# Loading the layer-normed x of a block with its rows repeated by the DMA, in place of copies by ScalarE and GpSimd

## The chip, the cores and the metric

The kernel runs on one core of one Trainium2 chip. The metric is the device time of one execution in microseconds (us), so lower is better. Before the change it is 2559.25 us, the median of 3 runs (2558.43 to 2561.18).

## The reference

One layer norm feeds two branches, multi-head attention and a GEGLU feed-forward network; their product gates the output. All arrays are float32: x is 2048 tokens by D = 576, there are 32 heads of 18 elements, and the feed-forward width is F = 4608.

```python
xn = layernorm(x)
q, k, v = split(xn @ wqkv)                     # 32 heads of 18
s = (softmax(q k^T / sqrt(18)) v) @ wo         # branch A
g = silu((gelu(xn @ w_gate) * (xn @ w_up)) @ w_down)   # branch B
return x + s * g
```

## The kernel before

Float32 products are made of reduced-precision pieces: a tile is split into a high part and a low part (x = hi + lo), and a product takes hi*hi, lo*hi and hi*lo.

The 2048 tokens are cut into NB = 4 blocks of TB = 512. A **prologue** (to about 198 us) norms and transposes each block's x, splits it (hi, lo), projects q, k and v, and stores q, k, v and also the transposed x itself: `store_xt` (L273) writes block b to a DRAM array `xhs[b]`, shaped [2 (hi, lo), 576 features, 512 tokens], so a feature's 512 tokens are one run of 2 KB.

The **main part** consists of sections (`section`, L578). A section makes one tile of 128 gate columns and 128 up columns for one token block: 27 pairs of matmuls (9 chunks of 64 features, 3 products each). A pair uses the upper and the lower half of TensorE's rows at once: gate weights stand in partitions 0 to 63, up weights in 64 to 127, and since both halves multiply the same x, the x chunk must stand in both halves of the partitions (L431, `rr = slice(HR * a, HR * a + HR)`). Between the pairs stand the score matmuls of the attention (L814 and L861), behind them the sums over values (L878) and, after every second section, the down projection (L542). TensorE's order is written out by hand, and so is the order of SP's DMA queue in the main part; in the prologue a scheduler places everything except TensorE's work.

A token block lasts 36 sections. Its x stands in SBUF as six tiles `xd0_k` (hi) and `xd1_k` (lo), k = 0, 1, 2, each [128 partitions, 3 chunks, 512 tokens], 768 KB, with a single buffer. So at a block's end, in its last section, the next block's tiles are loaded as the old ones fall free: k = 0 behind pair 9, k = 1 behind pair 18, k = 2 behind pair 27 (hooks at L606 to L608, and L620). Pairs 0 to 8 of the next section need k = 0, pairs 9 to 17 need k = 1, pairs 18 to 26 need k = 2. There are three such block ends, at about 727, 1327 and 1928 us.

Before the change `load_xd` (L146) loads k = 0 and k = 1 into the lower 64 partitions only, and engines copy them to the upper 64: ScalarE the hi tiles, GpSimd the lo tiles (`copy_xd`, L157). For k = 2 the load is issued twice, once for each half. Block 0 is loaded in the prologue, lower halves only, and GpSimd copies all six tiles (L388 to L391).

All DMAs are issued by SP, in order, on one queue. Each carries one of eight completion counters in turn, so SP can issue a request only when the request eight places ahead of it has landed.

Two other places matter below. In the prologue `project` (L314) writes its result to tiles t1 and t2 with three buffers, which SP stores to DRAM (`qk<-t`, L321), from a PSUM tile `po` with three buffers. And `load_scale` (L702) loads sums of the softmax with four rows of DRAM, each repeated for 32 partitions:

```python
o, d = spare()
nc.sync.dma_start(o[:, i, 0:TB], oT[g, :, cols])
nc.sync.dma_start(d[:, i, 0:TB], rT[QD * g:QD * g + QD, cols].rearrange("h (o s) -> h o s", o=1).to_broadcast([QD, 32, TB]))
```

The first fills 128 partitions from 128 rows, the second fills 128 partitions from 4 rows; each lands 256 KB.

Of the kernel before, what the change touches and what calls it, by code (L numbers as in the profile page):

```python
# [8 lines left out]
F32 = mybir.dt.float32  # L9
F32R = mybir.dt.float32r  # L10
AF = mybir.ActivationFunctionType
# [5 lines left out]
S, D, H, DH, F = 2048, 576, 32, 18, 4608  # L17
P = 128
NT = S // P
TB = 512  # L20
NB = S // TB
KT = 4
R0 = KT * P
HR = 64
NC = D // HR
XG = 3
NG = NC // XG
# [41 lines left out]
def gu_part(n):  # L69
    return G * part(*divmod(n // G, NR)) + n % G  # L70


def f(ap):
    return ap.bitcast(F32)
# [14 lines left out]
def kernel(ctx: ExitStack, tc: tile.TileContext, x, wqkv, wo, w_gate, w_up, w_down, out):  # L89
    nc = tc.nc  # L90
    x = x.rearrange("b s d -> (b s) d")
# [3 lines left out]
    dram = ctx.enter_context(tc.tile_pool(name="dram", bufs=1, space=DRAM))  # L95
# [9 lines left out]
    ys = dram.tile([S - TB, D], F32, name="ys")  # L105
    zeros = dram.tile([2, 2 * TB], F32, name="zeros")
    ts = dram.tile([NR, P, 2 * 7 * DC], F32, name="ts")
    xhs = [dram.tile([2, D, TB], F32, name=f"xhs{b}") for b in range(NB)]

    ident = const.tile([P, P], F32, name="ident")  # L110
    make_identity(nc, ident)
# [31 lines left out]
        w[1].append(hi)  # L143
        w[2].append(lo)

    def load_xd(b, k, halves=1):  # L146

        out = []
        for i in range(2):
            t = wts.tile([P, XG, TB], F32R, name=f"xd{i}_{k}")  # L150
            for a in range(halves):
                nc.sync.dma_start(f(t)[HR * a:HR * a + HR],
                                  xhs[b][i, k * XG * HR:(k + 1) * XG * HR, :].rearrange("(k p) t -> p k t", p=HR))
            out.append(t)
        return out

    def copy_xd(x, part, keep=lambda i: i, i=slice(None)):  # L157

        if part == 0:
            keep(nc.scalar.activation(x[0][HR:P, i], f(x[0])[0:HR, i], AF.Copy))  # L160
        else:
            keep(nc.gpsimd.tensor_copy(x[1][HR:P, i], x[1][0:HR, i]))


    def after(what, before, reason):
        tc.add_manual_dep(what.ins, before.ins.name, mybir.DependencyInfo(
            mybir.DependencyClass.Sync, mybir.DependencyReason.DATA), reason=reason)
# [7 lines left out]
    with tc.tile_pool(name="pro", bufs=1) as pro, tc.tile_pool(name="pps", bufs=1, space=PSUM) as pps:  # L175
# [34 lines left out]
        def load_x(b):  # L210
            keep = tc.keep_in_program_order if b == 1 else lambda i: i
            xr = []
            for j in range(4):
                xx = pro.tile([P, D + HR], F32, name="xx", bufs=4)
                keep(nc.sync.dma_start(xx[:, 0:D], x[b * TB + j * P:b * TB + (j + 1) * P, :]))
                xr.append(xx)
            return xr
# [43 lines left out]
        def transposes(b, xr):  # L261
            xt = XT[b % 2]
            pts = [pps.tile([P, TB], F32, name="pt", bufs=KT + 1) for k in range(KT + 1)]
            for j in range(4):
                if b == 0 and j == 0:
                    warm(46)
                for k in range(KT + 1):
                    nc.tensor.transpose(pts[k][:, j * P:(j + 1) * P], xr[j][:, k * P:(k + 1) * P], ident)  # L268
            for k in range(KT + 1):
                split_t(pts[k], k, xt)  # L270
            return xt

        def store_xt(b, xt):  # L273
            keep = tc.keep_in_program_order if b == 0 else lambda i: i
            for i in range(2):
                keep(nc.sync.dma_start(xhs[b][i, 0:R0, :].rearrange("(k p) t -> p k t", p=P), f(xt[i])))
                keep(nc.sync.dma_start(xhs[b][i, R0:D, :], f(xt[2])[HR * i:HR * i + HR, :]))

        XT = [(pro.tile([P, KT, TB], F32R, name=f"xth{i}"), pro.tile([P, KT, TB], F32R, name=f"xtl{i}"),
               pro.tile([P, TB], F32R, name=f"xtr{i}")) for i in range(2)]  # L280
# [10 lines left out]
        def load_qk(t, keep=lambda i: i):  # L291
            return t, load_rows(t * P, P, keep)
# [4 lines left out]
        def split_qk(t, raw):  # L297
            hi, lo = (pro.tile([P, KT, P], F32R, name=f"q{m}{t}") for m in "hl")
            first = split(hi, lo, raw)
            put_qk(t, hi, lo)  # L300
            return first
# [31 lines left out]
        t = ORDER[0]  # L333
# [26 lines left out]
        xt = transposes(0, xr)  # L360
        for c0 in (slice((t + 1) * P, 2 * D), slice(0, t * P)):
            split_av(QR[0][:, c0], QR[1][:, c0], raw_r[:, c0], tc.keep_in_program_order)
        for b in range(NB):
            for n, t in enumerate(ORDER):
                if b == 0 and n == 1:
                    nc.sync.dma_start(zeros.rearrange("i x -> (i x)").rearrange("(p x) -> p x", p=P), zz)
                if n == (2 if b == 0 else 0) and b + 1 < NB:
                    xr = load_x(b + 1)
                if b == 0 and ahead_qk:
                    first = split_qk(*ahead_qk.pop(0))  # L370
                    if n < 3:
                        after(first, last, "VectorE alone on the first x")
                    if n + 4 < NQT:
                        ahead_qk.append(load_qk(ORDER[n + 4]))
                if b == 0 and n == 4:
                    raw_r, VR = load_rest(2 * D, D)
                    split_av(VR[0], VR[1], raw_r, tc.keep_in_program_order)
                if b == 0 and n in (5, 6):
                    raw_v.append(load_wv(n - 5))
                if b == 0 and n in (7, 8):  # L380
                    split_wv(n - 7, raw_v[n - 7])
                project(b, t, xt)
                if n == 4 and b + 1 < NB:
                    norm(xr, b + 1)
            store_xt(b, xt)
            nxt = transposes(b + 1, xr) if b + 1 < NB else None
            if b == 1:
                XD = [load_xd(0, k) for k in range(NG)]  # L388
                for xd in XD:
                    for t in xd:  # L390
                        nc.gpsimd.tensor_copy(t[HR:P], t[0:HR])  # L391
            if b == 2:
                ahead = load_gu(0, tc.keep_in_program_order)
                for k in range(NG):
                    split_gu(ahead, k)
            for j in range(4):
                for c in range(2):
                    values_of(b, j, c, xt)
            xt = nxt
# [5 lines left out]
    FF = {"w": ahead, "xd": XD, "down": [], "gates": [], "n": 0, "hooks": {}, "raw": {},  # L405
          "M": ffn.tile([P, 7, 2, DC], F32, name="M"),
          "A": [ffn.tile([P, 7, TH], F32R, name=m) for m in ("ah", "al")],
          "T": ffn.tile([P, 2, 7, DC], F32R, name="T")}
# [169 lines left out]
    def section(specials=(), tag="f", slots=False):  # L578

        n = FF["n"]  # L580
        FF["n"] += 1
        b, r = divmod(n // G, NR)
        g = n % G
        keep = tc.keep_in_program_order
        pairs, pg, pu = gate_up(tag)
        hooks, FF["hooks"] = FF["hooks"], {}

        def hook(i, what):
            hooks.setdefault(i, []).append(what)

        for i in range(n + 1, min(n + 3, NF)):
            if i not in FF["raw"]:
                FF["raw"][i] = load_gu(gu_part(i))
        nxt = FF["raw"].pop(n + 1, None)
        one = split_ap if n + 1 < ATT.start else split
        if nxt:
            for k in range(NG - 1):
                split_gu(nxt, k, one)
        if n == 0:
            load_rawd(0)  # L600
        if g == 0 and (b, r) in FORMED:
            raw = FF["rawd"]
            hook(12, lambda: sums_b(raw))
        new = n + 1 < NF and (n + 1) % (NR * G) == 0
        xd = []
        if new:  # L606
            for k in range(NG - 1):
                hook(9 * k + 9, lambda k=k: xd.append(load_xd(b + 1, k)))  # L608
        for p in spread(pairs, specials, 1 if slots else None, hooks):
            p()  # L610
        if nxt:
            split_gu(nxt, NG - 1, one)
        FF["w"] = nxt
        if new:
            copy_xd(xd[0], 0, keep)
        FF["act"] = activate(pg, pu, g, n < ATT.stop)
        if g > 0 or n not in ATT:
            FF.pop("last", lambda: None)()
        if new:
            xd.append(load_xd(b + 1, NG - 1, 2))  # L620
            for t in hooks.get(len(pairs), ()):
                t()
            for i in range(XG):
                FF["hooks"].setdefault(2 + 2 * i, []).append(lambda i=i: copy_xd(xd[1], 0, keep, i))
            for k in range(NG - 1):
                for i in range(XG):
                    copy_xd(xd[k], 1, keep, i)
            FF["xd"] = xd

    def downs(then={}):  # L630
# [123 lines left out]
    with tc.tile_pool(name="att", bufs=1, reuse_waits="tile") as att:  # L754
# [180 lines left out]
        for n in range(NU * NA):  # L935
            u, i = divmod(n, NA)
# [7 lines left out]
            if FF["n"] % G == 1 and SCALED <= n < NU * NA - 2 and 2 < FF["n"] % (NR * G) < NR * G - 2:  # L944
                done = scaled + gated
                if (scaled + 1) * NA + 4 < n:
                    jobs, k = (load_scale, scale, store_scale), scaled
                    scaled += 1
                else:
                    jobs, k = (load_gate, gate, store_gate), gated  # L950
# [20 lines left out]
    with tc.tile_pool(name="epi", bufs=1, reuse_waits="tile") as epi:  # L971
# [173 lines left out]
        for m in ("rawd", "tsum"):  # L1145
            t = ffn.tile([P, 2, D], F32, name="xxs", tag=m)
# [33 lines left out]
        for i, c, m in QUARTERS:  # L1180
            t = ffn.tile([P, 2, DC], F32, name="tg", tag=("h0", "h1")[c], bufs=2 - c)
# [34 lines left out]
```

## Time and profile before

| what | us |
|---|---|
| median of 3 runs | 2559.25 |
| the profiled execution | 2558.65 |
| its span in the trace | 2556.6 |
| TensorE busy | 2540.1 (99%) |
| VectorE busy | 2089.0 (82%) |
| GpSimd busy | 1644.7 (64%) |
| ScalarE busy | 1462.6 (57%) |

The profiled execution took 2558.65 us, 2 us more than its span. In its views PE is TensorE (PEld its weight loads), DVE is VectorE, ACT is ScalarE, POOL is GpSimd and SPq the DMA queue of SP. An arrow "<-" stands between what an instruction writes and what it reads; in brackets stands the idle time ahead of it and whom it waited for. The DMA share is the mean busy share of the core's 16 DMA engines.

### The profile page before, as it was taken

To read this page: it belongs to the slowest core of one execution; us is meant where nothing else is said; L and a number is where in the kernel's file an instruction comes from. 1 tells how busy PE (TensorE), PEld (TensorE's weight loads), DVE (VectorE), ACT (ScalarE), POOL (GpSimd) and SP (SyncE) were. 2 spreads that over 40 slices of the span, in tenths; PEclk is the share of its full clock that TensorE was granted. 3 is DMA by queue.
4 is the path that set the end of the run, shared out by engine and by line. 5 is a ranking of instruction groups with operands and counts; after the bars stand their busy time and mean duration, and the time that the engine had idled before them with its cause. 6 is when DMAs were issued, how large, how long until landed. Compare 5 with 4: busy or idle time off the path is not lost.

```text
span 2556.6 us, 52908 instructions
## 1 busy us (share of the span) xinstructions
PE 2540.1 (99%) x20548; PEld 1840.8 (72%) x20548; DVE 2089.0 (82%) x2364; ACT 1462.6 (57%) x1765; POOL 1644.7 (64%) x1714
## 2 busy tenths in 40 slices
PE   9999999999999999999999999999999999999999
PEld 8888866676667766666666666766666776666788
DVE  5326888989888888888887889889898888888367
ACT  3224366666666665566666556555566665556631
POOL 3105588888888875666667566666667666666773
PEclk9999999999999999999999999999999999999999
DMA  8854455555585565677787677666668666665775
GB/s 259 273 187 134 106 165 160 167 168 158 162 220 162 167 172 142 163 169 169 169 194 192 162 169 168 174 168 157 160 159 213 164 173 172 163 167 153 190 212 209
DMA packets 410321, 446.88 MB, mean 175 GB/s; under 512 B 107092, under 2 KB 287060, under 8 KB 410072
## 3 DMA queue, kind: packets, MB, share of 16 engines
q1 hardware_dynamic: 410072, 443.50, 65.4%
q8 instruction: 164, 2.69, 0.5%
q14 instruction: 85, 0.70, 0.1%
HBM read 347.30 MB, written 96.08 MB: 173 GB/s over the span
## 4 chain that ended last, share of the span: by engine, by line
PE 97%; DVE 1%; POOL 1%; ACT 0%; DMA 0%; issue 0%; SPq 0%; POOLq 0%; DVEq 0%; ACTq 0%
PE pg L431 25%; PE acc L878 18%; PE py L542 15%; PE pm L814 9%; PE pe L861 9%; PE pu L431 9%; PE po L196 7%; PE po L1032 2%; PE pgu L431 1%; PE py L529 1%; DVE mx L815 0%; PE pt L268 0%; DMA rawp<-in_A_wqkv_dram 0%; POOL wl L124 0%; ACT pT L862 0%
## 5 line engine op out<-in xcount | busy, mean ns | idle before, releaser
L862 ACT ACTIVATE pT<-pe 128x1024 f32<-128x1024 f32 x1024 | 1048.1, 1027 | 572.7 <-PE pe L861 539.6
L815 DVE TENSOR_REDUCE mx<-pm 128x2 f32<-128x1024 f32 x1024 | 1220.2, 1224 | 166.5 <-PE pm L814 150.5
L431 PE MATMUL pu<-xd,wh 64*128 64x512 f32 x2466 | 902.2, 396 | 0.0
L431 PE MATMUL pg<-xd,wh 64*128 64x512 f32 x2466 | 901.3, 396 | 0.0
L431 PEld LDWEIGHTS pg<-xd,wh 64*128 64x128 f32 x2466 | 455.0, 185 | 114.4 <-issue 55.6
L431 PE MATMUL pg<-xd,wl 64*128 64x512 f32 x1233 | 481.4, 390 | 1.1 <-POOL wl L124 1.1
L431 PE MATMUL pu<-xd,wl 64*128 64x512 f32 x1233 | 481.6, 391 | 0.0
L431 PEld LDWEIGHTS pu<-xd,wh 64*128 64x128 f32 x2466 | 455.0, 184 | 17.5 <-ACT xd L160 0.2
L878 PE MATMUL acc<-pT,VS 128*32 128x512 f32 x4096 | 466.0, 595 | 0.0
L117 POOL TENSOR_SCALAR wh<-raw 128x384 fp32r<-128x384 f32 x402 | 218.7, 546 | 372.9 <-PE pu L431 262.0
L119 POOL TENSOR_TENSOR wl<-raw,wh 128x384 fp32r<-128x384 f32 x402 | 415.8, 1036 | 28.5
L814 PE MATMUL pm<-KA,QT 64*128 64x512 f32 x2048 | 413.7, 395 | 6.4 <-ACT pT L862 3.3
L861 PE MATMUL pe<-QT,KA 64*128 64x512 f32 x2048 | 411.0, 392 | 0.0
L542 PE MATMUL py<-T,ah 128*128 128x288 f32 x1876 | 380.6, 298 | 0.0
L549 DVE TENSOR_TENSOR M<-py,M 128x576 f32<-128x576 f32 x448 | 339.6, 758 | 31.7 <-PE py L542 18.1
L542 PEld LDWEIGHTS py<-T,ah 128*128 128x128 f32 x1876 | 298.4, 188 | 54.0 <-issue 54.0
L460 POOL TENSOR_TENSOR al<-h,ah 128x512 fp32r<-128x512 f32 (+1 forms) x143 | 295.6, 2067 | 61.5 <-ACT ah L457 51.7
L878 PEld LDWEIGHTS acc<-pT,VS 128*32 128x32 f32 x4096 | 120.1, 109 | 276.8 <-issue 229.7
L542 PE MATMUL py<-T,al 128*128 128x288 f32 x938 | 275.7, 294 | 0.0
L861 PEld LDWEIGHTS pe<-QT,KA 64*128 64x128 f32 x2048 | 192.9, 184 | 109.7 <-DVE mx L815 24.4
L431 PEld LDWEIGHTS pg<-xd,wl 64*128 64x128 f32 x1233 | 227.6, 185 | 36.4 <-POOL wl L124 2.0
L814 PEld LDWEIGHTS pm<-KA,QT 64*128 64x128 f32 x2048 | 198.9, 185 | 54.6 <-ACT pT L862 9.3
(174 smaller groups left out, 3001.7 us busy)
## 6 DMA issues: line engine op xcount, KB each, us to landing
T<-ts SPq DMA_DIRECT2D x98, 576.0 KB
KA<-qk SPq DMA_DIRECT2D x768, 72.0 KB
T<-ts SPq DMA_DIRECT2D x98, 432.0 KB
raw<-in_B_w_gate_dram SPq DMA_DIRECT2D x144, 288.0 KB
raw<-in_B_w_up_dram SPq DMA_DIRECT2D x144, 288.0 KB
ts<-T SPq DMA_DIRECT2D x36, 576.0 KB
VS<-vs SPq DMA_DIRECT2D x128, 152.0 KB
qk<-t SPq DMA_DIRECT2D x72, 256.0 KB
```

The source lines that it names most:

```text
L117: first = nc.gpsimd.tensor_scalar(hi, raw, 1.0, 1.0, op0=ALU.mult, op1=ALU.mult)
L119: keep(nc.gpsimd.tensor_tensor(lo, raw, f(hi), op=ALU.subtract))
L196: nc.tensor.matmul(o, st, m, start=(i == 0), stop=(i == len(terms) - 1))
L431: nc.tensor.matmul(o, w[1 + wp][k][rr, c, :], xd[k][xp][rr, c, :], start=(i == 0), stop=(i == len(terms) - 1))
L460: keep(two.tensor_tensor(lo, raw, f(hi), op=ALU.subtract))
L542: nc.tensor.matmul(py[:, t, 0:DC], h[:, i, tt], T[:, w, k], start=n == 0, stop=n == 2)
L549: nc.vector.tensor_tensor(M[:, m], py[:, :, 0:DC], M[:, m], op=ALU.add)
L814: nc.tensor.matmul(pm[:, a], QS[u, r][rr, t * P:(t + 1) * P], KS[(u * NA + c) % KB][r][rr, :], start=True, stop=True)
L815: nc.vector.tensor_reduce(MX[u][:, 2 * r:2 * r + 2, t, c], pm, axis=AX.X, op=ALU.max)
L861: nc.tensor.matmul(pe[:, a], KS[(u * NA + c) % KB][r][rr, t * P:(t + 1) * P], QS[u, r][rr, :], start=True, stop=True)
L862: nc.scalar.activation(PT[u, kt][:, 2 * r:2 * r + 2, :], pe, AF.Exp, scale=SCALE)
L878: nc.tensor.matmul(ACC[u][32 * a:32 * a + 32, :], VS[(u * NA + c) % VB][:, v:v + 32], pt[:, a, :], start=first, stop=last, skip_group_chec ...
```

## The change

A block's x is written to DRAM in another layout: [2, 64, 9 chunks x 512 tokens], so that what one partition of a tile needs is one run of 6 KB. Each of a block's six tiles is then loaded by one request that fills all 128 partitions: its source repeats the 64 rows twice (a leading dimension of size 2 with step 0). No engine copies x any more. The store takes six requests in place of four.

```diff
-    xhs = [dram.tile([2, D, TB], F32, name=f"xhs{b}") for b in range(NB)]
+    xhs = [dram.tile([2, HR, NC * TB], F32, name=f"xhs{b}") for b in range(NB)]
...
-    def load_xd(b, k, halves=1):
+    def load_xd(b, k):
         out = []
         for i in range(2):
             t = wts.tile([P, XG, TB], F32R, name=f"xd{i}_{k}")
-            for a in range(halves):
-                nc.sync.dma_start(f(t)[HR * a:HR * a + HR],
-                                  xhs[b][i, k * XG * HR:(k + 1) * XG * HR, :].rearrange("(k p) t -> p k t", p=HR))
+            rows = xhs[b][i, :, k * XG * TB:(k + 1) * XG * TB].rearrange("(o p) x -> o p x", o=1)
+            nc.sync.dma_start(f(t).rearrange("p k t -> p (k t)"), rows.to_broadcast([2, HR, XG * TB]))
             out.append(t)
         return out
-
-    def copy_xd(x, part, keep=lambda i: i, i=slice(None)):
-
-        if part == 0:
-            keep(nc.scalar.activation(x[0][HR:P, i], f(x[0])[0:HR, i], AF.Copy))
-        else:
-            keep(nc.gpsimd.tensor_copy(x[1][HR:P, i], x[1][0:HR, i]))
...
             for i in range(2):
-                keep(nc.sync.dma_start(xhs[b][i, 0:R0, :].rearrange("(k p) t -> p k t", p=P), f(xt[i])))
-                keep(nc.sync.dma_start(xhs[b][i, R0:D, :], f(xt[2])[HR * i:HR * i + HR, :]))
+                to = xhs[b][i].rearrange("p (c t) -> p c t", t=TB)
+                for a in range(2):
+                    keep(nc.sync.dma_start(to[:, a:NC - 1:2], f(xt[i])[HR * a:HR * a + HR]))
+                keep(nc.sync.dma_start(to[:, NC - 1], f(xt[2])[HR * i:HR * i + HR, :]))
...
                 XD = [load_xd(0, k) for k in range(NG)]
-                for xd in XD:
-                    for t in xd:
-                        nc.gpsimd.tensor_copy(t[HR:P], t[0:HR])
...
-        if new:
-            copy_xd(xd[0], 0, keep)
...
-            xd.append(load_xd(b + 1, NG - 1, 2))
+            xd.append(load_xd(b + 1, NG - 1))
...
-            for i in range(XG):
-                FF["hooks"].setdefault(2 + 2 * i, []).append(lambda i=i: copy_xd(xd[1], 0, keep, i))
-            for k in range(NG - 1):
-                for i in range(XG):
-                    copy_xd(xd[k], 1, keep, i)
```

What SP issues in the prologue, before: the loads of block 0 (`xd`, from `xhs_78`) stand spread between the stores of the projections of block 1 (`qk<-t`).

```order
L152 DMA xd_0_1002<-xhs_78 64x3x512
L321 DMA qk<-t_822 128x512
L321 DMA qk<-t_823 128x512
L321 DMA qk<-t_843 128x512
L321 DMA qk<-t_844 128x512
L152 DMA xd_0_1004<-xhs_78 64x3x512
L321 DMA qk<-t_894 128x512
L321 DMA qk<-t_895 128x512
L152 DMA xd_1_1006<-xhs_78 64x3x512
L321 DMA qk<-t_915 128x512
```

The same place after the change:

```order
L314 DMA qk<-t_960 128x512
L269 DMA xhs_79<-xtl_98 64x4x512
L270 DMA xhs_79<-xtr_99 64x512
L152 DMA xd_0_1006<-xhs_78 128x1x1536
L152 DMA xd_0_1008<-xhs_78 128x1x1536
L152 DMA xd_1_1010<-xhs_78 128x1x1536
L152 DMA xd_1_1012<-xhs_78 128x1x1536
L152 DMA xd_2_1014<-xhs_78 128x1x1536
L152 DMA xd_2_1016<-xhs_78 128x1x1536
L322 DMA vs<-vn_100 128x304
```

The six loads now stand in one run behind block 1's last `qk` store; eight `vs` stores, then the four loads of block 3's x (`xx`), then the `qk` stores of block 2 follow them.

On VectorE, in the prologue after the change, where block 2's projections (`t<-po`) meet the statistics of block 3's x (`bs<-xx`):

```order
L199 TENSOR_TENSOR xtr_96<-pt,xtr_96 64x512
L312 TENSOR_TENSOR t_1178<-po,t_1177 128x512
L312 TENSOR_TENSOR t_1199<-po,t_1198 128x512
L312 TENSOR_TENSOR t_1220<-po,t_1219 128x512
L216 BN_STATS bs<-xx 128x6 x3
L220 BN_AGGR st<-bs 128x2
```

Three projections now stand ahead of the statistics of x; before, all of the norm stood ahead of the first of them.

On SP at the second block end, before:

```order
L487 DMA T<-ts 128x864
L152 DMA xd_0_16556<-xhs_80 64x3x512
L152 DMA xd_0_16558<-xhs_80 64x3x512
L152 DMA xd_1_16599<-xhs_80 64x3x512
L152 DMA xd_1_16601<-xhs_80 64x3x512
L152 DMA xd_2_16655<-xhs_80 64x3x512 x2
L152 DMA xd_2_16658<-xhs_80 64x3x512 x2
L487 DMA T<-ts 128x1152
L487 DMA T<-ts 128x864
L782 DMA KA<-qk 18x2x512 x6
```

And after:

```order
L477 DMA T<-ts 128x864
L152 DMA xd_0_16546<-xhs_80 128x1x1536
L152 DMA xd_0_16548<-xhs_80 128x1x1536
L152 DMA xd_1_16589<-xhs_80 128x1x1536
L152 DMA xd_1_16591<-xhs_80 128x1x1536
L152 DMA xd_2_16644<-xhs_80 128x1x1536
L152 DMA xd_2_16646<-xhs_80 128x1x1536
L477 DMA T<-ts 128x1152
L477 DMA T<-ts 128x864
L765 DMA KA<-qk 18x2x512 x6
```

Eight requests of 64 partitions became six of 128; what stands ahead of them and behind them is the same.

## The prediction

> **What bounds the kernel now.** I read the busy times of the page first, then the chain that ended last, then that chain in order of time around one block end.
>
> ```profile
> PE 2540.1 (99%) x20548; PEld 1840.8 (72%) x20548; DVE 2089.0 (82%) x2364; ACT 1462.6 (57%) x1765; POOL 1644.7 (64%) x1714
> PE 97%; DVE 1%; POOL 1%; ACT 0%; DMA 0%; issue 0%; SPq 0%; POOLq 0%; DVEq 0%; ACTq 0%
> ```
>
> TensorE is busy 99% of the span and makes 97% of the chain. Work taken off ScalarE and GpSimd is therefore worth only what it costs TensorE where TensorE waits, and anything new that makes TensorE wait costs its full length. The chain in order of time shows where a section ends, because the value sums (acc) come directly behind its 27 pairs:
>
> ```profile
> 711.75 5.74 PE py L542 x42
> 727.66 3.57 PE acc L878 x32
> 743.05 3.57 PE acc L878 x32
> 762.58 3.57 PE acc L878 x32
> 776.36 3.57 PE acc L878 x32
> ...
> 1343.19 3.57 PE acc L878 x32
> ...
> 1947.10 5.74 PE py L542 x42
> ```
>
> From 762.58 to 776.36, an ordinary pair of sections, are 13.78 us; from 727.66 to 743.05, across the first block end, 15.39. The block end costs **1.6 us** now. The chain shows the same at the other two, so some **5.0 us** in all is what the copies, and the loads ahead of them, can give back.
>
> **What the new request costs.** No request of before has a leading dimension of 2, so I bound it by the requests that the trace has. The DMA share in half-microsecond windows says how many of the 16 engines a request keeps busy. In the first window only full-width requests run (128 rows of 4608 bytes), in the second only those of keys and queries (18 rows outermost), in the last three only the load of `od` from 4 rows repeated 32 times each:
>
> ```profile
> core 0: us, PE busy (x) PEld busy (x) DVE busy (x) ACT busy (x) POOL busy (x), PEclk, DMA share, GB/s
> 1918.00:1918.50 0.50, 0.50 (x5) 0.43 (x7) 0.47 (x1) 0.00 (x0) 0.00 (x0) 1.00 1.05 424
> 203.00:203.50 0.50, 0.50 (x8) 0.42 (x6) 0.00 (x0) 0.00 (x0) 0.50 (x2) 1.00 0.55 168
> 2339.50:2340.00 0.50, 0.50 (x8) 0.32 (x6) 0.50 (x2) 0.50 (x1) 0.42 (x2) 1.00 0.25 94
> 2340.00:2340.50 0.50, 0.50 (x8) 0.46 (x6) 0.50 (x1) 0.20 (x1) 0.50 (x1) 1.00 0.27 102
> 2340.50:2341.00 0.50, 0.50 (x8) 0.42 (x6) 0.50 (x1) 0.38 (x1) 0.50 (x2) 1.00 0.26 98
> ```
>
> The last column is GB/s, the one before it the share. A request with 4 outermost rows holds a share of 0.25, which is 4 engines of 16, for as long as it runs, and moves 98 GB/s; 18 outermost give 0.55, about 9 of 16, which is 18's largest divisor up to 16; 128 give all. The outermost count of a request sets how many engines carry it, and repeating rows inside does not widen it. The new load's outermost dimension is the repetition, **2**. I read from this: 2 engines, a share of 0.125.
>
> An engine moves 98 / 4 = 24.5 GB/s with rows of 2 KB and 424 / 16 = 26.5 (25.2 when divided by the share of 1.05) with rows of 4.6 KB. For rows of 6 KB I take the nearer row's middle, 25.7, so two engines move 51.4 GB/s and one load of 786,432 bytes takes **15.3 us** (14.8 at 26.5, 16.0 at 24.5). Six loads of a block take 91.8 us, in a line, since they use the same two engines.
>
> The rows alone leave another reading open, that a repeating source moves 98 GB/s however many rows lead. The Trainium skill speaks to it, and against the change: its page "DMA: Bandwidth & Descriptors", under "Why a DMA increments its semaphore by 16 and not by 1", says that the largest number up to 16 dividing the slowest dimension of both sides sets the engines, and under "Rules for kernel authors" that a leading zero-stride broadcast of c copies confines a DMA to at most c engines. By this, 2; the rows agree for 4 and 18, none of them has a 2. By it the sum is the one below; by the other reading it is that of the second rival.
>
> **Block ends.** The loads go out when they go out now, since what frees the tiles is unchanged:
>
> ```profile
> 720.74 1.25 SPq L152 DMA_DIRECT2D xd<-xhs  x2
> 723.98 1.31 SPq L152 DMA_DIRECT2D xd<-xhs  x2
> ...
> 1320.76 9.03 SPq L152 DMA_DIRECT2D xd<-xhs  x8
> ...
> 1921.28 9.02 SPq L152 DMA_DIRECT2D xd<-xhs  x8
> ```
>
> From issue to the first byte I take 2.5 us. The bounds are 2.1, from a load of 288 KB in the prologue (issued 98.78, used 101.58, rows below, less 0.7 of data), and 4.2, from the lo tile of k = 0 (first issue 720.74, used at 726.92, less 2.0 of data for two loads); an idle queue is nearer the first.
>
> ```profile
> 726.92 1.72 POOL L162 CAST xd<-xd 64x512 fp32r<-64x512 f32 x3 [2.08 <-DMA xd<-xhs]
> ```
>
> The last lo tile so lands at 1320.76 + 2.5 + 91.8 = 1415.1 at the second block end. Pairs 20 to 26 need it; 27 pairs take 727.66 - 717.49 = 10.2 us, so those seven take 2.6, and the section ends at 1417.7 where it ended at 1343.19: **+74.5**. At the third, 1921.28 + 96.9 = 2018.2 against 1947.10 - 3.57 = 1943.5: **+74.7**. At the first, two stores of T stand between the loads:
>
> ```profile
> ts<-T SPq DMA_DIRECT2D x36, 576.0 KB
> ts<-T SPq DMA_DIRECT2D x36, 432.0 KB
> ```
>
> Their 1008 KB take 2.5 us of every engine at 424 GB/s: 820.1 against 743.05, **+77.1**. The 5.0 us of the copies are inside these differences. TensorE waits in its own order, so everything behind it (scores, values, down projection) shifts with it.
>
> What queues behind? SP issues a request only when the one eight places ahead has landed, and it waits for it:
>
> ```profile
> SPq L782 <- DMA xd<-xhs: 18.3, 14, 1.7
> SPq L789 <- DMA T<-ts: 41.7, 29, 2.3
> ```
>
> The first row is the load of keys waiting for x, which it does not read, eight places behind. With loads of 15 us, the six KA loads, VS and the next weights behind them come out one per landing, and their own data pass the same two engines behind x. They end up to some 8 us behind the last x tile. The weights go to the section after next and KA is seven chunks ahead, so I price this at nothing; the cover is the section of 10.2 us and its value sums of 3.57. Without it a few us per block end would come on top.
>
> **The prologue.** Block 0's six loads go out in one run, behind the last `qk` store of block 1, and ahead of eight `vs` stores, the four loads of block 3's x and the `qk` stores of block 2.
>
> ```profile
> 90.78 1.04 SPq L321 DMA_DIRECT2D qk<-t  x2
> ...
> 98.78 0.38 SPq L215 DMA_DIRECT2D xx<-in_A_x_dram  x1
> ```
>
> ```profile
> 101.58 0.82 DVE L225 BATCH_NORM_STATS2 bs<-xx 128x6 f32<-128x288 f32 x2 [5.83 <-DMA xx<-in_A_x_dram]
> 102.43 0.21 DVE L229 BATCH_NORM_AGGREGATE st<-bs 128x2 f32<-128x12 f32 x1
> 111.20 0.69 DVE L319 TENSOR_TENSOR t<-po,t 128x512 fp32r<-128x512 f32 x1 [0.43 <-ACT t L318]
> ```
>
> ```profile
> 107.06 1.08 PE L196 MATMUL po<-xth,qh 128*128 128x512 f32 x4
> ...
> 126.66 1.09 PE L196 MATMUL po<-xth,qh 128*128 128x512 f32 x4
> ```
>
> With two more stores of xhs behind 91.8, the first load goes out at about 92.9, and the last lands at 92.9 + 2.5 + 91.8 = 187.2. The eighth `vs` store stands eight places behind the last load and waits for it; x of block 3 goes out behind it, at 187.8, and is used 2.8 us later, at 190.6. VectorE has done three projections of block 2 by then and stands at the statistics of x: 4 x (0.82 + 0.21) = 4.1, then 0.65 for the reciprocal and its wait, then the fourth projection's low part, 0.69: 196.0. TensorE has meanwhile done six projections (three PSUM buffers beyond the three that VectorE emptied) and stopped at 107.06 + 6 x 3.27 = 126.66, where the seventh began. **+69.3**.
>
> **Restart.** After long gaps TensorE may start slowly; the profile's one cold start is its first:
>
> ```profile
> 1.39 7.69 PE L259 MATMUL po<-ident 128*128 128x128 f32 x46 [1.39 <-POOL ident masks.py:199]
> ...
> 89.95 2.35 PE L268 MATMUL pt<-ident,xx 128*128 128x128 f32 x20
> ```
>
> 46 transposes took 167 ns each there, against 117 later, 2.3 us lost. Between 0 and 2.3 for each of four gaps I take 1.5, 6 in all. (The Trainium skill, "TensorE: Matmul & The Clock Gate", Part 1, has half clock for about 3.4 us after an idle window; by that 1.7 a gap, 7 in all. These gaps lie in no trace yet.)
>
> **Nothing elsewhere.** By the view of the tile xd, these copies go:
>
> ```profile
> L162 POOL CAST xd<-xd x18: 604/610/1152, 726.9 to 1934.0; 64x512 fp32r<-64x512 f32 x18
> L391 POOL CAST xd<-xd x6: 1461/1464/1472, 80.1 to 99.6; 64x1536 fp32r<-64x1536 f32 x6
> ```
>
> Three times six of 0.61 us on GpSimd, as many chunks on ScalarE, and six of 1.46 in the prologue, where x is first used at 198. The stores of x move the same bytes in six requests for four. The copies stood beside TensorE's work but for the 1.6 us of each block end.
>
> **Sum** against the profiled execution's 2558.65 (0.6 below the median): 77.1 + 74.5 + 74.7 + 69.3 + 6 = 301.6, **2860 us**.
>
> **Rivals.**
> - *Wide loads, not slower.* If a request of 128 partitions is spread by its destination, all 16 engines carry it, a load takes 2.0 us at 392 GB/s (16 x 24.5), a block's six are there when their pairs come, and the 1.6 us per block end come back: 2558.65 - 5.0 = 2553.7. It decides wherever the share during the loads is near 1. Against it: `od` also fills 128 partitions, and holds 0.25.
> - *98 GB/s whatever leads.* 8.0 us a load, 48.1 for six, 43.7 less at each of four places: 2860 - 175 = 2685. Against it: 0.25 is exactly four engines of rows that lead by four.
> - *Slower engines.* Keys and queries moved 168 GB/s on 0.55, 19 to 21 GB/s per engine by 9 engines or by the share; at 20 a load takes 19.7 us, 26 more at each place: 2860 + 105 = 2965. For it: both engines read the same rows. Against it: those requests are 36 rows each, with gaps.
> - *The prologue's gap hidden.* If the stores or x of block 3 find another way past the loads, 69 go: 2790. Against it: they stand in SP's one order.
>
> **Numbers.** Forecast 0.74 (its own range 2825 to 2910), wide 0.06, 98 GB/s 0.06, slower engines 0.08, hidden prologue 0.06. The range takes in the hidden prologue and the lower half of slower engines, 2788 to 2940, about 0.84; leaving out either would drop below 0.8. Faster or slower means by over 0.2%, about what a measurement of this kernel can tell from no change: 2553.7 lies on that bound, so wide is halved, faster 0.03, same 0.03; slower 0.94.
>
> **What would show it.** A DMA share near 0.13 for tens of us at four places (92 to 187, and three times behind a block end); gaps of TensorE that end with the landing of `xd`, about 15 us apart; SPq L765 waiting for `xd` 10 us and more; no L160 or L162. A share near 1 during the loads would refute the main step, two engines; a gap in the prologue that ends much before 187 would refute the queue behind it.

## The result and the profile after

The changed kernel takes **2866.99 us** (median of 5 runs, 2864.45 to 2870.44), against 2559.77 for the kernel before in the same comparison (5 runs): the ratio is 1.1201, 95% interval [1.1189, 1.1213]. It is 12% slower; 2860 was forecast, with a range of 2788 to 2940.

The page of the changed kernel, its busy times and the shares of the chain that ended last:

```profile
PE 2569.6 (90%) x20548; PEld 1859.3 (65%) x20548; DVE 2086.1 (73%) x2364; ACT 1453.7 (51%) x1753; POOL 1623.7 (57%) x1690
PE 82%; DMA 8%; SPq 3%; another core or an unknown queue 2%; POOL 2%; DVE 1%; issue 1%; ACT 0%; POOLq 0%; DVEq 0%; ACTq 0%
```

TensorE made 97% of the chain and makes 82% now. Its 29.5 us more of busy time are a slower clock, not more work: there are 20548 matmuls as before, and the granted clock is 0.54 to 0.67 in the gaps (windows below). What it waits for stands in the view of the waits (total us, times, longest one), from which these rows are taken:

```profile
PE pg L421 <- DMA xd<-xhs: 209.5, 18, 14.2
...
DVE bs L216 <- DMA xx<-in_A_x_dram: 76.4, 4, 74.2
...
PE po L187 <- DVE t L312: 71.7, 1, 71.7
```

The first row is the three block ends: 18 waits for a landing of `xd`, up to 14.2 us each. The other two are one gap in the prologue: VectorE waits 74.2 us for block 3's x, and TensorE 71.7 us for VectorE. Windows over the four gaps (the last three columns are TensorE's granted clock, the DMA share and GB/s):

```profile
core 0: us, PE busy (x) PEld busy (x) DVE busy (x) ACT busy (x) POOL busy (x), PEclk, DMA share, GB/s
100.00:187.00 87.00, 27.33 (x142) 23.14 (x141) 2.08 (x3) 3.86 (x8) 0.00 (x0) 0.67 0.16 64
813.00:890.00 77.00, 15.27 (x64) 9.99 (x64) 7.36 (x6) 6.14 (x6) 1.50 (x2) 0.54 0.16 62
1476.00:1565.00 89.00, 21.98 (x136) 13.32 (x132) 14.34 (x14) 12.42 (x14) 11.32 (x11) 0.61 0.18 65
2155.00:2243.00 88.00, 22.20 (x130) 13.60 (x126) 13.90 (x13) 11.79 (x14) 11.32 (x11) 0.61 0.18 65
```

TensorE idles most of the time, and yet the DMA engines are not busy either: a share of 0.16 to 0.18, with the little else that runs beside the loads. That is the mark of few engines, not of many bytes.

To see where the 308.6 us of span went, I compared the start and end of each section (its 54 matmuls on `xd`) in the two traces. The prologue is read behind the third section, a block end from the section before it to the third one behind it. The same table holds for the experiments below (us against the kernel before):

| kernel | prologue | first end | second | third | rest | span |
|---|---|---|---|---|---|---|
| the change | 75.2 | 77.9 | 77.6 | 76.8 | 1.1 | 308.6 |
| e1 halves | 3.7 | 8.2 | 6.3 | 7.5 | -0.3 | 25.4 |
| e2 twice | 24.6 | 0.8 | -1.9 | -1.6 | 2.6 | 24.5 |
| e3 lead2 | 80.4 | 80.6 | 79.2 | 78.3 | 2.0 | 320.5 |
| e4 first only | 71.5 | 6.3 | 7.3 | 7.1 | -1.4 | 90.8 |
| e5 lead4 | 45.7 | 35.6 | 35.1 | 35.7 | -0.4 | 151.7 |
| e6 lower | -1.2 | 0.0 | 0.0 | 0.0 | 0.2 | -1.0 |
| e7 columns | 20.8 | 4.1 | -1.7 | -1.5 | 2.6 | 24.3 |
| e8 copied in DRAM | -1.1 | 1.0 | -1.7 | -1.5 | 0.9 | -2.4 |

### The profile page after: what moved, and what is told of

Its sections match the earlier page's. It is cut to its first block, busy times and chain, and to the rows that moved or that the text cites. A ratio compares the mean times of both kernels' runs of the same rounds, so it can differ in the third digit from the quotient of the medians.

```text
span 2865.2 us, 52876 instructions
## 1 busy us (share of the span) xinstructions
PE 2569.6 (90%) x20548; PEld 1859.3 (65%) x20548; DVE 2086.1 (73%) x2364; ACT 1453.7 (51%) x1753; POOL 1623.7 (57%) x1690
## 4 chain that ended last, share of the span: by engine, by line
PE 82%; DMA 8%; SPq 3%; another core or an unknown queue 2%; POOL 2%; DVE 1%; issue 1%; ACT 0%; POOLq 0%; DVEq 0%; ACTq 0%
PE pg L421 21%; PE acc L861 15%; PE py L532 13%; PE pu L421 8%; PE pm L797 8%; PE pe L844 8%; DMA xd<-xhs 7%; PE po L187 5%; SPq L152 2%; PE py L519 1%; PE po L1015 1%; PE pgu L421 1%; DMA vs<-vn 1%; SPq L322 1%
## 5 line engine op out<-in xcount | busy, mean ns | idle before, releaser
L421 PE MATMUL pg<-xd,wh 64*128 64x512 f32 x2466 | 914.8, 401 | 209.5 <-DMA xd<-xhs 209.5
L421 PE MATMUL pu<-xd,wh 64*128 64x512 f32 x2466 | 915.6, 401 | 0.0
L421 PEld LDWEIGHTS pg<-xd,wh 64*128 64x128 f32 x2466 | 460.9, 187 | 333.3 <-issue 129.6
L421 PEld LDWEIGHTS pu<-xd,wh 64*128 64x128 f32 x2466 | 460.8, 187 | 18.7
L421 PEld LDWEIGHTS pu<-xd,wl 64*128 64x128 f32 x1233 | 231.0, 187 | 9.6
```

Of the source, the lines that this page charges most:

```text
L421: nc.tensor.matmul(o, w[1 + wp][k][rr, c, :], xd[k][xp][rr, c, :], start=(i == 0), stop=(i == len(terms) - 1))
```

## The experiments

My theory: the leading count of 2 puts each load on two of the 16 engines, and four times the kernel waits for 4.72 MB to pass through them. The rivals: the new layout with its 6 KB rows is slow by itself; reading the same rows twice is slow, whatever leads; or the prologue and the block ends aren't independent.

### e1 and e2: the same layout without the leading 2

e1 loads each tile in two requests of 64 partitions (4 runs):

```diff
-            rows = xhs[b][i, :, k * XG * TB:(k + 1) * XG * TB].rearrange("(o p) x -> o p x", o=1)
-            nc.sync.dma_start(f(t).rearrange("p k t -> p (k t)"), rows.to_broadcast([2, HR, XG * TB]))
+            for a in range(2):
+                rows = xhs[b][i, :, k * XG * TB:(k + 1) * XG * TB]
+                nc.sync.dma_start(f(t)[HR * a:HR * a + HR].rearrange("p k t -> p (k t)"), rows)
```

> The new layout of x in DRAM and its 6 KB rows are kept, no engine copies x, but each tile comes by two requests of 64 rows, one for each half of the partitions, with nothing repeated. Theory (the leading 2 of the request puts it on two engines): 64 leading rows go on all 16 engines, a half lands in 384 KB / 410 GB/s = 1.0 us, a block's twelve in about 12 us, the gaps of TensorE at the four places go, and the 1.6 us of each block end come back at least in part: 2553 to 2560 us. Rival (the layout, rows 18 KB apart in DRAM, is slow to read): the loads stay long and the time stays above 2800.

e2 stores every row twice, so that one request reads 128 real rows (5 runs):

```diff
-    xhs = [dram.tile([2, HR, NC * TB], F32, name=f"xhs{b}") for b in range(NB)]
+    xhs = [dram.tile([2, P, NC * TB], F32, name=f"xhs{b}") for b in range(NB)]
...
+            rows = xhs[b][i, :, k * XG * TB:(k + 1) * XG * TB]
+            nc.sync.dma_start(f(t).rearrange("p k t -> p (k t)"), rows)
...
+                for h in range(2):
+                    to = xhs[b][i, HR * h:HR * h + HR].rearrange("p (c t) -> p c t", t=TB)
```

> As the changed kernel, one request of 128 partitions for each tile, but the store writes every row of x to DRAM twice, so that the request reads 128 rows of their own and repeats none: its leading dimension is 128. Theory: 16 engines, 2.0 us a tile, no gaps, 2553 to 2562 us (the prologue writes 4.5 MB more). Rival (one request for 128 partitions with 6 KB rows is slow as such, or SP's issue of it is): above 2800.

Measured: e1 **2584.04 us** (ratio to 2558.58 for the kernel before on the same chip 1.0099 [1.0084, 1.0115]), e2 **2579.65** (1.0081 [1.0068, 1.0094]). In both the gaps of 70 to 80 us are gone, with the same layout in DRAM; so the layout isn't the cause. But they missed their ranges by 24 and 18 us, and the table says that they lose in different places: e1 loses 6 to 8 us at each block end, e2 nothing there, but 24.6 in the prologue, where it stores twice as much: 9.4 MB more, not the 4.5 of its expectation. e7, e6 and e8 take these apart.

### e3 and e4: the leading count without the repetition, and one place alone

e3 repeats nothing. The 64 rows lie in DRAM in two groups of 32 with a gap between them, and each half tile is a request whose source leads with 2 (a single run):

```diff
-    xhs = [dram.tile([2, HR, NC * TB], F32, name=f"xhs{b}") for b in range(NB)]
+    xhs = [dram.tile([2, 2, 32 + 1, NC * TB], F32, name=f"xhs{b}") for b in range(NB)]
...
+            for a in range(2):
+                rows = xhs[b][i, :, 0:32, k * XG * TB:(k + 1) * XG * TB]
+                nc.sync.dma_start(f(t)[HR * a:HR * a + HR].rearrange("p k t -> p (k t)"), rows)
```

> As the two-requests kernel, nothing repeated, but the rows of x lie in DRAM in two groups of 32 with a row left free between them, so that a request's source has a leading dimension of 2 (2 groups of 32 rows), and the store takes twice as many requests. Theory (the leading count alone, not the repetition, sets two engines): a half takes 32 rows x 0.234 us = 7.5 us on two engines, a tile 15, and the time is that of the changed kernel, 2840 to 2890 us. Rival (the repetition, the same rows read by two engines at a time, is what is slow): no gaps, 2555 to 2575 us.

e4 repeats rows for block 0 alone and loads the other blocks as e1 does (a single run):

```diff
+            if b == 0:
+                rows = xhs[b][i, :, k * XG * TB:(k + 1) * XG * TB].rearrange("(o p) x -> o p x", o=1)
+                nc.sync.dma_start(f(t).rearrange("p k t -> p (k t)"), rows.to_broadcast([2, HR, XG * TB]))
+            for a in range(2 * (b > 0)):
+                rows = xhs[b][i, :, k * XG * TB:(k + 1) * XG * TB]
+                nc.sync.dma_start(f(t)[HR * a:HR * a + HR].rearrange("p k t -> p (k t)"), rows)
```

> The repeating request is kept for block 0 in the prologue alone; blocks 1 to 3 come by two requests of 64 rows. Theory (the four places add up): the prologue's 75.2 us of the changed kernel stay, the three block ends lose nothing: 2555 + 75 = 2630, 2622 to 2640 us, with the first sections 75 us later than before and the end 75 us later. Rival (the prologue's gap belongs to the order in which SP's requests stand after the change, not to the loads): it stays in the two-requests kernel as well, and this one is no slower than that.

Measured: e3 **2878.88 us**, all four gaps back. Windows of e3 in the prologue and at the first block end:

```profile
100.00:170.00 70.00, 25.32 (x127) 21.14 (x126) 2.08 (x3) 3.45 (x7) 0.00 (x0) 0.71 0.13 51
830.00:880.00 50.00, 14.10 (x51) 8.59 (x50) 4.91 (x4) 5.12 (x5) 1.50 (x2) 0.50 0.15 61
```

The share is 0.13 without any repetition: the leading count alone does it, and reading the same rows twice is not what is slow. e4 took **2649.25 us**: 71.5 us in the prologue, and at the block ends 6 to 7, much as e1. Its prologue loses 3.7 us less than that of the changed kernel, mostly because the last load lands earlier (187.0 for 188.9 us) and because the first projection behind the gap takes 4.94 us for 6.11. Within such few us the places add up; one doesn't hide or cause another. Its expectation was missed by 9 us, because I had not yet put e1's loss at the block ends into it.

### e5: a leading count of 4

As e3, with four groups of 16 rows (a single run):

```diff
-    xhs = [dram.tile([2, 2, 32 + 1, NC * TB], F32, name=f"xhs{b}") for b in range(NB)]
+    xhs = [dram.tile([2, 4, 16 + 1, NC * TB], F32, name=f"xhs{b}") for b in range(NB)]
...
-                rows = xhs[b][i, :, 0:32, k * XG * TB:(k + 1) * XG * TB]
+                rows = xhs[b][i, :, 0:16, k * XG * TB:(k + 1) * XG * TB]
```

> Nothing is repeated; the rows lie in four groups of 16, so that each request of 64 partitions leads with 4. By the leading count 4 engines carry each request, a share of 0.25; a block's 4.72 MB take 44.9 us at 26.3 GB/s per engine instead of the 89.7 of two engines, so each of the four gaps of 77 to 81 us shrinks by 44.8 to 32 to 36: 2680 to 2705 us. If the leading count were a switch (few rows ahead are slow, however many), the time stays near 2870.

Measured: **2710.12 us**. Windows of e5 in the prologue and at the first block end:

```profile
105.00:135.00 30.00, 21.18 (x96) 16.99 (x95) 2.08 (x3) 2.37 (x5) 0.00 (x0) 0.94 0.28 104
790.00:805.00 15.00, 6.54 (x24) 3.90 (x25) 2.45 (x2) 1.93 (x3) 1.51 (x2) 0.61 0.29 113
```

The share doubles to 0.28, the rate to 104 GB/s, and the block ends fall from 78 to 81 us to 35.1 to 35.7, inside what was expected of them. In the prologue the requests of 384 KB land 3.74 us apart, 105 GB/s, 26.3 per engine. The total is 5 us over its range, and that is the prologue: 45.7 us where 32 to 36 were expected. Its grouped layout stores a block in 24 requests for 6, and the first load goes out at 104.7 us instead of 94.3.

### e6 and e7: what e1 lost

e6 is the kernel before, copies and all, with the new layout alone (11 runs):

```diff
-    xhs = [dram.tile([2, D, TB], F32, name=f"xhs{b}") for b in range(NB)]
+    xhs = [dram.tile([2, HR, NC * TB], F32, name=f"xhs{b}") for b in range(NB)]
...
-                nc.sync.dma_start(f(t)[HR * a:HR * a + HR],
-                                  xhs[b][i, k * XG * HR:(k + 1) * XG * HR, :].rearrange("(k p) t -> p k t", p=HR))
+                nc.sync.dma_start(f(t)[HR * a:HR * a + HR].rearrange("p k t -> p (k t)"),
+                                  xhs[b][i, :, k * XG * TB:(k + 1) * XG * TB])
```

> The kernel before with the new layout in DRAM alone: the lower 64 partitions come in 6 KB rows, and ScalarE and GpSimd copy them to the upper half as before. If the loss of the halves kernel (25 us) came from its doubled loads, this one stands within 0.2% of before: 2554 to 2563 us. If the layout itself or its six stores cost something, it keeps part of the loss: 2565 to 2584.

e7 is e2 with two requests per tile, cut by columns instead of by partitions: as many requests and bytes as e1, but each over all 128 partitions (a single run):

```diff
+            N = XG * TB // 2
+            for a in range(2):
+                rows = xhs[b][i, :, k * XG * TB + N * a:k * XG * TB + N * a + N]
+                nc.sync.dma_start(f(t).rearrange("p k t -> p (k t)")[:, N * a:N * a + N], rows)
```

> The kernel with rows stored twice, but each tile loaded by two requests of 128 partitions and half the columns (3 KB rows). As many requests and bytes as with halves, at full width. If the halves lost 6 to 8 us at each block end because their requests are twice as many, this loses them too: 2596 to 2604. If it was the 64-partition width that made them slow, block ends cost nothing, as with one request: 2577 to 2583.

Measured: e6 **2559.56 us** (1.0000 [0.9991, 1.0009]), e7 **2582.65**. So the layout costs nothing and brings nothing. e7's second and third block ends are e2's, not e1's (-1.7 and -1.5 against 6.3 and 7.5): it isn't the number of requests. The first end is the exception, 4.1 us against e2's 0.8, but most of that isn't the loads: over the first two sections behind the end e7 has lost 0.5 us; in the third TensorE waits 1.77 us for VectorE's maximum (0.79 in e2) and then runs at a granted clock of 0.50 from 796.7 to 800.1 us. Here is one stretch of the loads at the first block end, first of e1, then of e7:

```profile
738.00:742.00 4.00, 2.07 (x11) 0.96 (x10) 1.35 (x2) 1.53 (x2) 3.86 (x3) 1.00 1.00 283
```

```profile
754.00:758.00 4.00, 4.00 (x38) 3.08 (x36) 3.86 (x4) 3.42 (x4) 3.83 (x4) 1.00 1.03 416
```

Both have all engines busy (1.00 and 1.03), but e1 moves 283 GB/s and e7 416. In both some 107 to 110 GB/s of it are rows of T over all 128 partitions (127 packets of 3456 bytes in e1, 124 in e7); what is left for the loads of x is 174 in e1 and 309 in e7. The same is seen where e6 loads its lower halves, in the second of these stretches with nothing beside them:

```profile
95.00:99.00 4.00, 4.00 (x32) 4.00 (x31) 0.00 (x0) 1.06 (x3) 0.00 (x0) 1.00 1.04 238
99.00:103.00 4.00, 4.00 (x32) 4.00 (x31) 0.00 (x0) 0.82 (x2) 3.18 (x3) 1.00 1.03 209
```

By the packet records a 6 KB row takes a median of 419 to 478 ns in e1 and e6, and 234 in e2 and in the block ends of e8, whose requests fill 128 partitions. The Trainium skill, "SBUF — State Buffer", section "Door 1: The DMA port swizzle (why `[64,N]` ≈ `[32,N]`)", says that 64 neighbouring partitions reach only 8 of 16 ports and gives about 218 GB/s as their limit; e6's 209 agrees, where its loads run alone; its 238 has 90 rows of 2 KB of another request in it. So e1 pays for width: at a block end it takes twelve requests of 384 KB where the kernel before took eight, all at about half the rate. TensorE waits 4.7, 4.1 and 4.6 us for `xd` at the three ends of e1, and its granted clock is half for 6.8, 3.4 and 6.8 us behind these waits. No run separates the partitions that are written from the rows that are read (64 different ones a request in e1, 128 in e7).

### e8: rows stored once, copied in DRAM

The prologue stores each row once; eight requests in the middle of a block copy the next block's rows from DRAM to DRAM, and a block end loads 128 real rows. Block 0 is loaded and copied by GpSimd as in the kernel before (11 runs; DUP is 12, so the copies stand in sections 12 to 19 of a block's 36):

```diff
+        j = n % (NR * G) - DUP
+        if 0 <= j < 8 and b + 1 < NB:
+            i, o = divmod(j, 4)
+            nc.sync.dma_start(xhs[b + 1][i, HR + 16 * o:HR + 16 * o + 16], xhs[b + 1][i, 16 * o:16 * o + 16])
...
+            w = HR if b == 0 else P
+            rows = xhs[b][i, 0:w, k * XG * TB:(k + 1) * XG * TB]
+            nc.sync.dma_start(f(t)[0:w].rearrange("p k t -> p (k t)"), rows)
```

> Rows stored once in the prologue; the second copy of blocks 1 to 3 is made from DRAM to DRAM in eight pieces of 590 KB in the middle of the block before, and block 0 is copied by GpSimd as before. If the 24 us of the twice-stored kernel are its stores in the prologue, they go, and what is left is what the engine copies cost at the block ends, 1 to 5 us in all: 2553 to 2559 us. If the copies from DRAM to DRAM delay the weights, 2560 to 2580.

Measured: **2556.97 us** against 2559.32 for the kernel before on the same chip, 0.9990 [0.9981, 0.9999]. The eight copies are 288 KB each, not the 590 of the expectation. e2's 24.6 us in the prologue are gone with the second store (e1, which stores once too, has 3.7 there). The loads of the first block end in e8:

```profile
726.00:730.00 4.00, 4.00 (x38) 1.13 (x36) 3.11 (x4) 2.12 (x5) 2.11 (x3) 1.00 1.03 425
730.00:734.00 4.00, 4.00 (x36) 3.15 (x36) 2.81 (x3) 3.62 (x4) 3.83 (x5) 1.00 1.01 419
```

All engines, 420 GB/s, TensorE busy in all of these 8 us. This is the fastest version of the study, by 2.4 us, which is little more than the noise (the interval ends at 0.9999): with the DMA doing the repetition at full width, that is all that is gained on the engine copies.

## Why the prediction was right, step by step

**What bounds the kernel.** Work off ScalarE and GpSimd would be worth only TensorE's waits at the block ends, 1.6 us each. e8 takes that work off: 1.7 and 1.5 us at the second and third end. At the first it lost 1.0 instead, so the 5.0 us in all were too high; 2.4 came. There TensorE still waits for the last tile of x, which goes out behind two stores of T, and two sections later for VectorE, which waits for GpSimd:

```profile
738.77 0.49 PE L428 MATMUL pg<-xd,wh 64*128 64x512 f32 x1 [1.27 <-DMA xd<-xhs]
...
769.49 0.21 DVE L825 STREAM_TRANSPOSE mt<-m 128x32 f32<-128x32 f32 x1 [1.07 <-POOL m L820]
...
770.86 0.50 PE L855 MATMUL pe<-QT,KA 64*128 64x512 f32 x2 [0.90 <-DVE mx L809]
```

As far as the trace tells, the second wait comes from GpSimd's order and not from the loads: without the copies three splits of weights (wh, wl) stand between its last `M` and this `m`, where before one stood. e2 and e7 have that order and that wait too; no run put the old order back.

**Two engines per load.** Right. Each load posts two completions, one of each engine, where those of e1, e2, e6, e7 and e8 post 16; e3 and e5 show that the leading count sets it, 2 and 4. The rule that the prediction cited, of the Trainium skill's "DMA: Bandwidth & Descriptors", section "Why a DMA increments its semaphore by 16 and not by 1", holds at 2, 4 and 64 or 128 here.

**15.3 us per load.** A little high: 14.95 between landings in the prologue, 26.3 GB/s per engine for 25.7 (the middle of the 25.2 and 26.5 that I had is 25.85, not 25.7, which changes the 15.3 by 0.1). The last two landings of the first block end are seen on TensorE of the changed kernel, 15.1 us apart, and so is what follows the second of them:

```profile
876.03 0.76 PE L421 MATMUL pg<-xd,wh 64*128 64x512 f32 x1 [11.75 <-DMA xd<-xhs]
...
891.13 0.79 PE L421 MATMUL pg<-xd,wh 64*128 64x512 f32 x1 [13.45 <-DMA xd<-xhs]
...
895.46 3.64 PE L861 MATMUL acc<-pT,VS 128*32 128x512 f32 x32
```

**Block ends.** +77.1, +74.5 and +74.7 forecast, before the restart; 77.9, 77.6 and 76.8 measured with it. With the 1.5 us that I gave each restart the sums are 78.6, 76.0 and 76.2. The last landing at the second end is at 1568.25 us; less the shift of 152.8 by then, that is 1415.5, where 1415.1 was forecast. That these are so near is partly luck: six loads of 14.95 us make 2.1 less than the 91.8 of the sum, and the last two landings there are 16.5 and 15.8 us apart, with rows of T and of keys on the engines between them, for which the sum had nothing. From issue to the first landing there are 17.6 us, 2.6 more than a load, as forecast (2.5).

**Restart.** Low. I took 1.5 us per gap. The seven last pairs take 891.13 to 895.46, 4.3 us for 2.6, so 1.7 lost; at the second end 5.0 (2.4 lost), at the third 4.2 (1.6):

```profile
1568.29 0.79 PE L421 MATMUL pg<-xd,wh 64*128 64x512 f32 x1 [14.05 <-DMA xd<-xhs]
...
1573.28 3.89 PE L861 MATMUL acc<-pT,VS 128*32 128x512 f32 x32
```

```profile
2246.56 0.79 PE L421 MATMUL pg<-xd,wh 64*128 64x512 f32 x1 [14.21 <-DMA xd<-xhs]
...
2250.73 3.64 PE L861 MATMUL acc<-pT,VS 128*32 128x512 f32 x32
```

In the prologue of the changed kernel the first projection behind the gap takes 6.11 us where the next takes 3.26:

```profile
199.05 2.08 PE L187 MATMUL po<-xth,qh 128*128 128x512 f32 x4 [71.72 <-DVE t L312]
...
205.16 1.09 PE L187 MATMUL po<-xth,qh 128*128 128x512 f32 x4
...
208.42 1.09 PE L187 MATMUL po<-xth,qh 128*128 128x512 f32 x4
```

That is 2.85 lost; 8.6 in the four gaps for 6. The granted clock shows it: it is half until 894.6, 1573.8, 2249.7 and 205.1 us.

**Prologue.** +69.3 forecast, and 70.8 with the restart; 75.2 measured, the largest miss. The order on SP was as forecast, but SP was held elsewhere. The queue of SP in the changed kernel:

```profile
94.30 61.12 SPq L152 DMA_DIRECT2D xd<-xhs  x6
155.53 33.76 SPq L322 DMA_DIRECT2D vs<-vn  x8
189.44 1.78 SPq L206 DMA_DIRECT2D xx<-in_A_x_dram  x4
```

And its part of the chain in order of time:

```profile
98.51 27.48 SPq L152
...
126.04 14.67 SPq L152
...
140.75 14.67 SPq L152
...
155.53 14.59 SPq L322
...
170.22 19.59 DMA vs<-vn
```

I had SP issue the six loads at once and the eighth store wait for the last of them. In fact the fourth load already holds SP for 27.48 us, inside the issue and not in a wait for a completion (the one that it needs had come at 92.2 us), and each of the next three requests for another 14.6, one per load that lands. It cost nothing more, because the last store still waits until the loads are done. The 4.4 us that were missing are: the last load landing at 188.9 us for 187.2 (the first goes out 1.4 us later than forecast and lands 19.9 us behind its issue, 4.9 more than a load where 2.5 was taken; against that six loads are 2.1 us shorter), x of block 3 going out with it at 189.44; its use 3.65 us later where I had 2.8; VectorE's way to the fourth projection, 0.5 more; and the restart, 1.35 more. VectorE waits for x as forecast:

```profile
193.09 1.18 DVE L216 BATCH_NORM_STATS2 bs<-xx 128x6 f32<-128x288 f32 x3 [74.21 <-DMA xx<-in_A_x_dram]
```

That SP's order makes this gap, and not x of block 0 itself (needed only behind the prologue), is read from the trace; no run moved the stores past the loads.

**What queues behind, at nothing.** Right. At the first end SP spends 20.66 us on the six KA loads, 14.65 of it inside the first one's issue, and comes to the next weights at 891.76, right behind the last landing; yet the two sections behind each block end stay within 0.4 us of its shift. At the second and third ends a KA load waits 10.7 and 10.9 us for `xd`. From the view of SP's waits, and its queue in order of time at the first end:

```profile
SPq L765 <- DMA xd<-xhs: 21.6, 2, 10.9
```

```profile
840.00 17.36 SPq L152 DMA_DIRECT2D xd<-xhs  x2
857.40 20.66 SPq L765 DMA_DIRECT2D KA<-qk  x6
...
891.76 0.65 SPq L137 DMA_DIRECT2D raw<-in_B_w_gate_dram  x1
```

**The sum.** 7.0 us low in 308.6: the three ends with their restarts are off by -0.7, +1.6 and +0.6, the prologue with its restart by +4.4, and 1.1 come in the rest, for which nothing was taken.

**The rivals.** "Wide" needed a share near 1; the share is 0.16 to 0.18, what else runs in the gaps included (e3's 0.13 in the prologue is the cleaner reading). "98 GB/s whatever leads" would have given 2685: a count of 4 does give 104 GB/s, and a count of 2 gives 51. "Slower engines" had 20 GB/s per engine: measured 26.3. "The prologue's gap hidden" had 2790: the gap is there.

## What to carry to other kernels

Read a DMA by its outermost dimension before reading its bytes: a repeat written as a leading dimension of 2 used two of 16 engines and took 15 us for 768 KB, which 128 real rows bring in 1.9 (between landings in e2). A low DMA share beside a wait for a DMA shows it at once. And before copies are moved to the DMA from engines that have time for them, read what they cost where the bound engine waits: here 2.4 us of 2559, all that the version gained which repeats the rows at full width.

## What the runs showed of the hardware that I had not expected

- SP is held inside a request's issue when few engines carry the ones ahead. With 2 engines per request and 768 KB each, three go out within 4.2 us, the fourth takes 27.48 us and the next two 14.67 each; with e3's 384 KB the fourth is the first one held, 6.2 us, and the next two 7.3 and 7.2; with four engines (e5) seven go out within 4.3 us, the eighth is held 8.4 and each of the next four some 3.5. What is full by then was not tried.
- Half the partitions get half the DMA rate: 209 GB/s into 64 (e6, from 99 to 103 us, with nothing beside it) against 419 to 425 into 128 (e8), with a share of 1.0 in both.
- TensorE's half rate behind a long gap (a matmul on `xd` takes 0.62 us for 0.39) lasted 3.5, 5.5 and 3.1 us at the block ends and 6.1 in the prologue, from the first matmul behind the gap to the end of the half granted clock. The Trainium skill, "TensorE: Matmul & The Clock Gate", Part 1, has about 3.4 us; two of the four are longer.
